# Attention and gated feed-forward in one kernel: the start of the first block in another order, with up weights loaded early

## The chip, the cores and the metric

The kernel runs on one core of a Trainium2 chip. The metric is device time in microseconds; the median of several executions counts. TensorE (PE) multiplies, VectorE (DVE) and ScalarE (ACT) do elementwise work and copy results out of PSUM, GpSimd (POOL) does masks and scaling, SyncE (SP) issues most of the DMAs.

## The reference, cut to what matters

One input x of 2048 tokens by 448 features is normalized, and the result feeds two branches: sliding-window attention with 16 heads of 28 features and a window of 256 tokens, and a gated feed-forward of width 1792. All tensors are bf16.

```python
xn = _layernorm(x)                       # x: (1, 2048, 448)
qkv = (xn @ wqkv)                        # wqkv: (448, 3 * 448), 16 heads of 28
scores = einsum("bhqd,bhkd->bhqk", q, k) * 28 ** -0.5
scores = where((i - j >= 0) & (i - j < 256), scores, -1e9)
attn = einsum("bhqk,bhkd->bhqd", softmax(scores), v) @ wo
ffn = (gelu(xn @ w_gate) * (xn @ w_up)) @ w_down      # w_gate, w_up: (448, 1792)
return x + attn + ffn
```

## The kernel before

The tokens are cut into 16 tiles of 128 and four blocks (`qb`) of 512. `stat(t)` takes mean and variance of a tile on DVE, `rstd(t, n)` the inverse deviation of n tiles on ACT (logarithm, then exponential), `norm(t)` writes the normalized tile `xn`. The transposed form `xnT` comes for tiles 0 to 3 from PE (`transp`: four transposes into PSUM and a copy), for later tiles from a DMA transpose issued by SP (`dma_transp`).

The 448 features are three chunks of 128 rows and a last one of 64. A product over them is therefore three dense matmuls (`mm3`) and one of half height (`mm_half`). `norm` writes the last 64 features twice, so that two half matmuls, of two different results, can run side by side in the upper and the lower half of the PE array. This text calls a stretch of half-height matmuls between dense ones an excursion.

Every block has an attention stage and a gated stage. In attention, each of four groups of heads has score steps (`sc`, four heads side by side, 32 rows each), an exponential of the scores on ACT into `p_sb`, masks on POOL (block 0) or DVE, and later the product with v (`ov`). Block 0 has twelve score steps, three in each group: 512, 384 and 256 columns of each head. The score pool has one buffer of four PSUM banks, so a score step waits until the exponential before it is done.

Between score steps PE is filled from `feeds`, lists of generators taken in order: `gen_qk` (q and k of a head group), `gen_v` (v of two tiles), `gen_proj` (all projections of the next block), `gen_up` (up products of two rows of 128 hidden features, `ue`, kept in hT until the gate is there). `bank()` gives these results PSUM banks in turn from a ring of tags: m (two banks) and d; tag o has one bank. A result's bank is free again when ACT or DVE has copied it out. `aux` holds one call after each score step, such as statistics of later tiles. The order of each engine's instructions is the order in which the program writes them; nothing is moved by a scheduler afterwards.

The first block starts with an order written out by hand: warm-up matmuls on zeros, the statistics, norms and transposes of tiles 0 to 3, v of tiles 0 and 1, q and k of group 0 in two halves of 256 tokens, v of tiles 2 and 3. Then the loop over blocks begins, and its first feed goes on with q and k of groups 1 to 3, the projections of block 1 and two up pairs (`early`).

The weights of q and k come by DMA as `wraw` and are copied by `pads` into `wqp` and `wkp`, where each head has 32 columns; the last 64 rows of q and k go to `w3p`. DMAs take one of eight completion semaphores in turn, so that a DMA issue waits until the one eight before it has landed. `loads()` issues the DMA transposes of tiles 4 to 7 and then the loads of up, gate, wo and down weights, after the second score step.

Of the kernel before, what the change touches and what calls it, by code (L numbers as in the profile page):

```python
# [12 lines left out]
f32 = mybir.dt.float32  # L13
# [3 lines left out]
P = 128  # L17
# [58 lines left out]
def kernel(  # L76
# [21 lines left out]
    def score_pool(n):  # L98

        if phase[0] is not None:  # L100
            phase[0].close()
        phase[0] = ExitStack()
        phase[0].pool = phase[0].enter_context(tc.tile_pool(name="sps", bufs=n, space=bass.MemoryType.PSUM))

    score_pool(1)
# [17 lines left out]

    nc.sync.dma_start(out=x_sb[:, 0, :], in_=xv[:, 0, :])
    nc.scalar.dma_start(out=x_sb[:, 1, :], in_=xv[:, 1, :])
    nc.sync.dma_start(out=x_sb[:, 2:4, :], in_=xv[:, 2:4, :])
    nc.sync.dma_start(out=wv[:, 0:3, :], in_=rows(A_wqkv, 0, 3)[:, :, 2 * D:3 * D])
    nc.scalar.dma_start(out=wraw[:, 0:3, :], in_=rows(A_wqkv, 0, 3)[:, :, 0:2 * D])
    for a in range(2):
        nc.sync.dma_start(out=wv[64 * a:64 * a + 64, 3, :], in_=A_wqkv[384:448, 2 * D:3 * D])  # L130
    for a in range(2):
        nc.sync.dma_start(out=wraw[64 * a:64 * a + 64, 3, 0:D], in_=A_wqkv[384:448, a * D:(a + 1) * D])
    nc.sync.dma_start(out=x_sb[:, 4:8, :], in_=xv[:, 4:8, :])

# [4 lines left out]
    nc.sync.dma_start(out=x_sb[:, 8:16, :], in_=xv[:, 8:16, :])  # L139
# [16 lines left out]
    make_masks()  # L156
# [20 lines left out]
    def warmup(n):  # L177
        wps = phase[0].pool.tile([P, 4, QB], f32, name="wps", tag="s")
        for i in range(n):
            nc.tensor.matmul(wps[:, i % 4, :], lhsT=warm[:, 0:P], rhs=warm[:, 0:QB], start=True, stop=True)  # L180
# [14 lines left out]
    def norm(t):  # L195
        xn = work.tile([P, 4, P], bf16, name="xn", bufs=4)
        xf = xn[:, :, :].rearrange("p a b -> p (a b)")
        for eng, lo, n, src in ((nc.vector, 0, D, 0), (nc.vector, D, 64, 384)):
            eng.tensor_scalar(out=xf[:, lo:lo + n], in0=x_sb[:, t, src:src + n], scalar1=mv_all[:, t, 0:1],
                              scalar2=rstd_all[:, t:t + 1], op0=ALU.subtract, op1=ALU.mult)  # L200
        xns[t] = xn
# [33 lines left out]

    def gen_v(qb, ts):

        for t in ts:
            pvs = []
            for i in range(2):  # L240
                pv = bank("pv")
                cs = slice((t + i) * P, (t + i + 1) * P)
                mm3(pv[:, 0:D], lambda c: xnT[:, c, cs], lambda c: wv[:, c, :], True, False)
                pvs.append(pv)
                yield (570, HOLD) if i else 570
            for i in range(2):
                mm_half(pvs[i][:, 0:D], xnT[:, 3, (t + i) * P:(t + i + 1) * P], wv[:, 3, :], i, False, True)
            for i in range(2):
                (nc.vector.tensor_copy if qb > 1 or i else nc.scalar.copy)(out=v_sb[:, t + i, :, 0:Dh], in_=pvs[i][:, 0:D].rearrange("p (h d) -> p h d", d=Dh))  # L249
            yield -360  # L250

    def gen_qk(qb, gs, lo=0, n=QB):

        ts = slice(qb * QB + lo, qb * QB + lo + n)
        for g in gs:
            hs = slice(4 * g, 4 * g + 4)
            pq = bank("pq")
            mm3(pq[:, 0:n], lambda c: wqp[:, c, hs, :].rearrange("p h d -> p (h d)"), lambda c: xnT[:, c, ts], True, False)
            yield 650
            pk = bank("pk")  # L260
            mm3(pk[:, 0:n], lambda c: wkp[:, c, hs, :].rearrange("p h d -> p (h d)"), lambda c: xnT[:, c, ts], True, False)
            yield 650, HOLD
            w3 = w3p[:, hs, :].rearrange("p h d -> p (h d)")
            mm_half(pq[:, 0:n], w3, xnT[:, 3, ts], 0, False, True)
            mm_half(pk[:, 0:n], w3, xnT[:, 3, ts], 1, False, True)
            nc.scalar.copy(out=qT[:, g, ts], in_=pq[:, 0:n])
            nc.vector.tensor_copy(out=kT[:, g, ts], in_=pk[:, 0:n])  # L267
            if lo + n == QB:
                done.add((qb, g))
            yield -360  # L270
# [67 lines left out]
    def gated(qb, early, last_v, hook):  # L338
# [5 lines left out]
        def begin(f):  # L344
            last_tag[0] = turn[0] if f not in early else last_tag[0]
            pr = dict(f=f, gt=phase[0].pool.tile([P, 2, QB], f32, name="gt", tag="s"), us=[])
            if f not in early:
                alone = (turn.pop(0), 1)
                tags = (("m", 2), alone)
                if qb == 0 and f == 0:  # L350
                    nxt = [ring[0][(ring[1] + i) % 3] for i in range(2)]
                    tags = [(x, 2 if x == "m" else 1) for x in nxt]
                for tag, n in tags:
                    pr["us"].append(psum.tile([P, QB], f32, name="u0", tag=tag, bufs=n))
            return pr
# [244 lines left out]
    warmup(10)  # L600
# [5 lines left out]
    transp(0, 1, nc.scalar.copy, "o")  # L606
    norm(1)
    warmup(1)
    transp(1, 1, nc.scalar.copy, "d")
    stat(2)  # L610
    stat(3)
    rstd(2, 2)
# [3 lines left out]
    norm(2)  # L616
    norm(3)
    run(gen_v(0, (0,)))
    qk = gen_qk(0, (0,), 0, 2 * P)
    next(qk)  # L620
    transp(2, 1, nc.scalar.copy, "o")
    transp(3, 1, nc.vector.tensor_copy, "m")
    stat(4)
    run(qk)
    stat(5)
    pads(nc.vector.tensor_copy, wqp, slice(1, 4))
    pads(nc.vector.tensor_copy, wkp, slice(1, 4))
    run(gen_qk(0, (0,), 2 * P, 2 * P))
    rstd(4, 2)
    stat(6)  # L630
    v23 = gen_v(0, (2,))
    next(v23)
    next(v23)
    norm(4)
    norm(5)
    stat(7)

    def loads():

        for t in range(4, 8):  # L640
            dma_transp(t)
        nc.sync.dma_start(out=wu[:, :, :], in_=rows(B_w_up, 0, 3))
        for t3, lo, hi in ((wgu3, B_w_gate, B_w_up), (wug3, B_w_up, B_w_gate)):
            nc.sync.dma_start(out=t3[0:64, :], in_=lo[384:448, :])
            nc.sync.dma_start(out=t3[64:128, :], in_=hi[384:448, :])
        for lo in (0, F // 2):
            nc.sync.dma_start(out=wg[:, :, lo:lo + F // 2], in_=rows(B_w_gate, 0, 3)[:, :, lo:lo + F // 2])
        wo_v = A_wo.rearrange("(g j d) n -> j d g n", g=4, j=4)
        for j in range(4):
            nc.sync.dma_start(out=wo[32 * j:32 * j + Dh, :, :], in_=wo_v[j])  # L650
        for k in range(0, NF, 3):
            n = min(3, NF - k)
            nc.sync.dma_start(out=wd[:, k:k + n, :], in_=rows(B_w_down, k, n))

    for qb in range(NB):
        early = ()
        aux, plan = [], {}
        if qb < 2:
            aux = [lambda: rstd(6, 2), lambda: (norm(6), norm(7), loads()), lambda: None] * (1 - qb) + [lambda t=t: stat(t) for t in range(8, 12)] * (1 - qb) + [lambda: rstd(4 * qb + 8, 4)]
        if qb == 0:  # L660
            new_hT(0)
            early = (2, 8)
            feeds = [Feed((v23, 360), (gen_qk(0, (1, 2, 3)), 3 * QK1), (gen_proj(1), PROJ), (gen_up(0, early), UP1 * len(early)))]
            feeds[0].held = True
# [12 lines left out]
        if qb:  # L677
            score_pool(1)
# [157 lines left out]
```

## Time and profile before

| | |
|---|---|
| median of 5 runs | 228.19 us (227.95 to 228.72) |
| profiled execution | 228.19 us |
| its span, first to last instruction | 226.2 us |
| PE, DVE, ACT, POOL busy | 217.1, 147.6, 133.4, 43.2 us |
| mean granted PE clock | 0.995 |
| DMA moved | 12.69 MB, 56 GB/s over the span |

The span leaves out some 2 us around the instructions. PE's busy time counts pipelined matmuls whose ends are modelled, so it can be 96% while PE still loses time between starts; the starts of its instructions tell more. A line number such as L218 is the line of the kernel, but helpers such as `mm3` record all their matmuls under one line, so the tile names (pv for v, pq and pk for q and k, sc for scores, ue and u for up, gt for gate, po for the output) tell which work it is.

### The profile page before, as it was taken

To read this page: it belongs to the slowest core of one execution; us is meant where nothing else is said; L and a number is where in the kernel's file an instruction comes from. 1 tells how busy PE (TensorE), PEld (TensorE's weight loads), DVE (VectorE), ACT (ScalarE), POOL (GpSimd) and SP (SyncE) were. 2 spreads that over 40 slices of the span, in tenths; PEclk is the share of its full clock that TensorE was granted. 3 is DMA by queue.
4 is the path that set the end of the run, shared out by engine and by line. 5 is a ranking of instruction groups with operands and counts; after the bars stand their busy time and mean duration, and the time that the engine had idled before them with its cause. 6 is when DMAs were issued, how large, how long until landed. Compare 5 with 4: busy or idle time off the path is not lost.

```text
span 226.2 us, 5435 instructions
## 1 busy us (share of the span) xinstructions
PE 217.1 (96%) x2262; PEld 97.0 (43%) x2262; DVE 147.6 (65%) x353; ACT 133.4 (59%) x129; POOL 43.2 (19%) x63
## 2 busy tenths in 40 slices
PE   6889999999999999999999999999999999999990
PEld 2433333344444444444444445444344435334470
DVE  5896887777675647588565656595444776679310
ACT  4578897524868876422868886333567775653000
POOL 8514777320000002222000002222000002222000
PEclk9999999999999999999999999999999999999997
DMA  6916999211200001001300100000000000100011
GB/s 215 328 28 74 313 311 308 74 23 31 44 0 24 25 5 41 6 0 38 59 0 23 24 4 25 23 0 0 0 4 23 22 5 5 42 3 0 22 45 26
DMA packets 18454, 12.69 MB, mean 56 GB/s; under 512 B 9784, under 2 KB 17784, under 8 KB 18424
## 3 DMA queue, kind: packets, MB, share of 16 engines
q1 hardware_dynamic: 17880, 11.48, 19.0%
q10 hardware_dynamic: 544, 0.80, 1.0%
q8 instruction: 19, 0.31, 0.6%
q14 instruction: 11, 0.09, 0.2%
HBM read 8.77 MB, written 1.84 MB: 47 GB/s over the span
## 4 chain that ended last, share of the span: by engine, by line
PE 86%; DVE 5%; ACT 2%; DMA 2%; SPq 1%; POOL 1%; issue 1%; DVEq 0%
PE po L301 19%; PE gt L218 16%; PE u L218 11%; PE po L296 6%; PE sc L539 6%; PE gt L223 5%; PE ov L501 4%; PE ue L218 4%; PE pq L218 4%; PE pk L218 4%; PE pv L218 3%; DMA wraw<-in_A_wqkv_dram 2%; PE pq L223 2%; POOL oN L451 1%; PE ue L223 1%; DVE st L185 1%
## 5 line engine op out<-in xcount | busy, mean ns | idle before, releaser
L543 ACT ACTIVATE p_sb<-sc 128x2048 bf16<-128x2048 f32 (+2 forms) x42 | 73.9, 1759 | 10.2 <-PE sc L539 8.5
L301 PE MATMUL po<-wd,hT 128*128 128x448 bf16 (+1 forms) x238 | 50.0, 342 | 0.0
L376 ACT ACTIVATE ge<-gt 128x1024 bf16<-128x1024 f32 x28 | 28.7, 1024 | 35.4 <-PE u L223 22.2
L218 PE MATMUL gt<-xnT,wg 128*128 128x512 bf16 x168 | 40.5, 380 | 0.0
L451 POOL TENSOR_TENSOR oN<-oc,rb 128x512 bf16<-128x512 f32 x10 | 12.7, 1269 | 118.0 <-DVE ri L480 62.1
L380 DVE TENSOR_TENSOR hT<-ge,u 128x512 bf16<-128x512 bf16 x42 | 26.9, 682 | 11.8 <-ACT ge L376 11.7
L218 PE MATMUL u<-xnT,wu 128*128 128x512 bf16 x126 | 30.6, 379 | 0.0
L301 PEld LDWEIGHTS <-hT 128*128 128x128 bf16 x238 | 21.6, 98 | 18.6 <-issue 2.2
L432 DVE TENSOR_TENSOR p_sb<-p_sb,masks 128x256 bf16<-128x256 bf16 (+1 forms) x90 | 24.6, 329 | 0.0
L218 PEld LDWEIGHTS <-wg 128*128 128x128 bf16 x168 | 15.1, 98 | 21.6 <-issue 5.4
L218 PEld LDWEIGHTS <-wu 128*128 128x128 bf16 x168 | 16.0, 98 | 19.2 <-issue 1.0
L507 DVE TENSOR_TENSOR oc<-oc,ov 128x512 f32<-128x512 f32 x12 | 8.3, 688 | 19.4 <-ACT oc L506 19.4
L539 PE MATMUL sc<-qT,kT 32*64 32x320 bf16 (+7 forms) x640 | 16.9, 263 | 0.4 <-ACT p_sb L543 0.3
L442 POOL TENSOR_SCALAR_AFFINE_SELECT p_sb<-p_sb 128x512 bf16<-128x512 bf16 (+1 forms) x20 | 14.2, 727 | 13.3 <-ACT p_sb L543 13.3
L306 DVE TENSOR_TENSOR res<-po,x_sb 128x448 bf16<-128x448 f32 (+1 forms) x17 | 9.9, 584 | 10.4 <-PE po L301 10.1
L296 PE MATMUL po<-wo,oN 128*128 128x448 bf16 (+1 forms) x68 | 16.3, 343 | 0.0
L267 DVE CAST kT<-pk 128x512 bf16<-128x512 f32 (+1 forms) x17 | 11.0, 648 | 7.8 <-PE pk L223 7.8
L506 ACT COPY oc<-ov 128x512 f32<-128x512 f32 x12 | 7.0, 585 | 15.2 <-POOL oN L451 12.8
L451 POOL TENSOR_TENSOR oN<-oc,l 128x512 bf16<-128x512 f32 x6 | 8.4, 1394 | 30.7 <-DVE l L468 30.7
L335 DVE CAST hT<-ue 128x512 bf16<-128x512 f32 x14 | 9.0, 686 | 7.1 <-PE ue L223 7.1
L223 PE MATMUL gt<-xnT,wgu 64*128 64x512 bf16 x49 | 13.6, 380 | 0.1
L218 PE MATMUL pq<-xnT,wqp 128*128 128x512 bf16 (+1 forms) x51 | 13.2, 368 | 0.2 <-DVE v_sb L249 0.2
(75 smaller groups left out, 236.4 us busy)
## 6 DMA issues: line engine op xcount, KB each, us to landing
out_dram<-res SPq DMA_DIRECT2D x15, 112.0 KB, 1.9
wu<-in_B_w_up_dram SPq DMA_DIRECT2D x1, 1344.0 KB
wg<-in_B_w_gate_dram SPq DMA_DIRECT2D x2, 672.0 KB, 9.6
wd<-in_B_w_down_dram SPq DMA_DIRECT2D x4, 336.0 KB, 7.3
x_sb<-in_A_x_dram SPq DMA_DIRECT2D x1, 896.0 KB, 5.8
wraw<-in_A_wqkv_dram ACTq DMA_DIRECT2D x1, 672.0 KB, 5.1
x_sb<-in_A_x_dram SPq DMA_DIRECT2D x1, 448.0 KB
wo<-in_A_wo_dram SPq DMA_DIRECT2D x4, 98.0 KB
```

The lines of the kernel that those rows point to most:

```text
L218: nc.tensor.matmul(ps, lhsT=lhs(c), rhs=rhs(c), start=start and c == 0, stop=stop and c == 2, skip_group_check=True)
L223: nc.tensor.matmul(ps, lhsT=lhs[p0:p0 + 64], rhs=rhs[p0:p0 + 64], start=start, stop=stop, tile_position=(p0, 0), skip_group_check=True)
L267: nc.vector.tensor_copy(out=kT[:, g, ts], in_=pk[:, 0:n])
L296: nc.tensor.matmul(po[:, 0:w], lhsT=oN[:, g, cs], rhs=wo[:, g, lo:up], start=(g == 0), stop=False, skip_group_check=True)
L301: nc.tensor.matmul(po[:, 0:w], lhsT=hT[:, f, cs], rhs=wd[:, f, lo:up], start=False, stop=(f == NF - 1), skip_group_check=True)
L376: nc.scalar.activation(out=ge[:, :, :], in_=pr["gt"][:, :, :], func=ACT.Gelu_apprx_tanh)
L380: nc.vector.tensor_tensor(out=hT[:, f + i, :], in0=ge[:, i, :], in1=u[:, :], op=ALU.mult)
L432: nc.vector.tensor_tensor(out=reg, in0=reg, in1=m, op=ALU.mult)
L442: nc.gpsimd.affine_select(out=reg, in_=reg, pattern=mid + [[1 if diag else -1, min(w, P)]], compare_op=ALU.is_ge, fill=0.0, base=0 if diag ...
L451: nc.gpsimd.tensor_tensor(out=oN[:, g, :], in0=oc[:, :], in1=inv, op=ALU.mult)
L539: nc.tensor.matmul(ss[k0:k0 + nk, j, col:col + nq], lhsT=kT[r, g, kt * P + k0:kt * P + k0 + nk], rhs=qT[r, g, qb * QB + q0:qb * QB + q0 + ...
L543: nc.scalar.activation(out=p_sb[:, :, 0:ncol], in_=ss[:, :, 0:ncol], func=ACT.Exp, scale=SCALE)
```

## The change

The start of block 0 is written in another order, and with it some loads and the score pool.

- v of a tile is put behind the transposes of the next one, with its dense part alone (`v_dense`). The half-height parts of q and k of group 0 and of v of tiles 0 and 1 stand together in one excursion; those of v of tiles 2 and 3 are added to the excursion of group 1's q and k.
- q and k of group 0 are computed for all 512 tokens at once, in the score pool, which begins as two buffers of two banks and becomes one of four when the scores begin.
- `rstd` runs for tiles 2 and 3 one by one; the second 64 features' copy of tiles 1 and 2 is written by POOL; `make_masks` comes later on POOL; eight warm-up matmuls open the kernel instead of ten.
- ACT's queue loads only group 0's columns of q and k; the others come on SP's queue, and the last rows of wraw go ahead of those of wv. Up weights are loaded ahead of x of tiles 8 to 11; x of tiles 12 to 15 and the gate, wo and down weights follow in `loads()`, some in fewer DMAs.
- Norms and transposes of tiles 4 to 7, and v's copies of tiles 2 and 3, are spread over the first score steps (`ahead`, `ahead2`, `ahead3`).
- One up pair stands ahead of block 1's projections in the feed, the other behind them.

```diff
-    score_pool(1)
+    score_pool(2)
...
+    wqk = rows(A_wqkv, 0, 3)[:, :, 0:2 * D]
     nc.sync.dma_start(out=x_sb[:, 0, :], in_=xv[:, 0, :])
     nc.scalar.dma_start(out=x_sb[:, 1, :], in_=xv[:, 1, :])
     nc.sync.dma_start(out=x_sb[:, 2:4, :], in_=xv[:, 2:4, :])
+    for c in (0, D):
+        nc.scalar.dma_start(out=wraw[:, 0:3, c:c + 4 * Dh], in_=wqk[:, :, c:c + 4 * Dh])
     nc.sync.dma_start(out=wv[:, 0:3, :], in_=rows(A_wqkv, 0, 3)[:, :, 2 * D:3 * D])
-    nc.scalar.dma_start(out=wraw[:, 0:3, :], in_=rows(A_wqkv, 0, 3)[:, :, 0:2 * D])
+    for a in range(2):
+        nc.sync.dma_start(out=wraw[64 * a:64 * a + 64, 3, 0:D], in_=A_wqkv[384:448, a * D:(a + 1) * D])
     for a in range(2):
         nc.sync.dma_start(out=wv[64 * a:64 * a + 64, 3, :], in_=A_wqkv[384:448, 2 * D:3 * D])
-    for a in range(2):
-        nc.sync.dma_start(out=wraw[64 * a:64 * a + 64, 3, 0:D], in_=A_wqkv[384:448, a * D:(a + 1) * D])
     nc.sync.dma_start(out=x_sb[:, 4:8, :], in_=xv[:, 4:8, :])
+    for c in (0, D):
+        nc.sync.dma_start(out=wraw[:, 0:3, c + 4 * Dh:c + D], in_=wqk[:, :, c + 4 * Dh:c + D])
...
-    nc.sync.dma_start(out=x_sb[:, 8:16, :], in_=xv[:, 8:16, :])
+    nc.sync.dma_start(out=wu[:, :, :], in_=rows(B_w_up, 0, 3))
+    nc.sync.dma_start(out=wug3[0:64, :], in_=B_w_up[384:448, :])
+    nc.sync.dma_start(out=wgu3[64:128, :], in_=B_w_up[384:448, :])
+    nc.sync.dma_start(out=x_sb[:, 8:12, :], in_=xv[:, 8:12, :])
...
-        for eng, lo, n, src in ((nc.vector, 0, D, 0), (nc.vector, D, 64, 384)):
+        for eng, lo, n, src in ((nc.vector, 0, D, 0), (nc.gpsimd if t in (1, 2) else nc.vector, D, 64, 384)):
...
+    def v_dense(t, pv):
+        mm3(pv, lambda c: xnT[:, c, t * P:(t + 1) * P], lambda c: wv[:, c, :], True, False)
+
+    def v_half(t, pv):
+        mm_half(pv, xnT[:, 3, t * P:(t + 1) * P], wv[:, 3, :], t % 2, False, True)
+
+    def v_copy(t, pv, copy):
+        copy(out=v_sb[:, t, :, 0:Dh], in_=pv.rearrange("p (h d) -> p h d", d=Dh))
...
+    def qk_halves(qb, g, pq, pk):
+        w3 = w3p[:, 4 * g:4 * g + 4, :].rearrange("p h d -> p (h d)")
+        for hi, ps in enumerate((pq, pk)):
+            mm_half(ps, w3, xnT[:, 3, qb * QB:(qb + 1) * QB], hi, False, True)
...
                     nxt = [ring[0][(ring[1] + i) % 3] for i in range(2)]
                     tags = [(x, 2 if x == "m" else 1) for x in nxt]
+                    if "d" in nxt:
+                        turn.insert(0, "o")
...
-    warmup(10)
+    warmup(8)
     stat(0)
     rstd(0, 1)
     stat(1)
     rstd(1, 1)
     norm(0)
     transp(0, 1, nc.scalar.copy, "o")
+    stat(2)
     norm(1)
+    rstd(2, 1)
     warmup(1)
     transp(1, 1, nc.scalar.copy, "d")
-    stat(2)
     stat(3)
-    rstd(2, 2)
+    rstd(3, 1)
+    pvs = [bank("pv")[:, 0:D]]
+    v_dense(0, pvs[0])
+    norm(2)
     pads(nc.vector.tensor_copy, wqp, slice(0, 1))
     nc.vector.tensor_copy(out=w3p[:, :, 0:Dh], in_=wraw[:, 3, 0:D].rearrange("p (h d) -> p h d", d=Dh))
     pads(nc.scalar.copy, wkp, slice(0, 1))
-    norm(2)
+    transp(2, 1, nc.scalar.copy, "o")
+    pvs.append(bank("pv")[:, 0:D])
+    v_dense(1, pvs[1])
     norm(3)
-    run(gen_v(0, (0,)))
-    qk = gen_qk(0, (0,), 0, 2 * P)
-    next(qk)
-    transp(2, 1, nc.scalar.copy, "o")
-    transp(3, 1, nc.vector.tensor_copy, "m")
+    make_masks()
+    transp(3, 1, nc.vector.tensor_copy, "d")
+    pvs.append(alone("pv", "o"))
+    v_dense(2, pvs[2])
+    pq, pk = (phase[0].pool.tile([P, 2, QB], f32, name="s0", tag="s")[:, 0, :] for _ in range(2))
+    proj(pq, wqp, 0, 0)
+    proj(pk, wkp, 0, 0)
     stat(4)
-    run(qk)
     stat(5)
-    pads(nc.vector.tensor_copy, wqp, slice(1, 4))
-    pads(nc.vector.tensor_copy, wkp, slice(1, 4))
-    run(gen_qk(0, (0,), 2 * P, 2 * P))
     rstd(4, 2)
-    stat(6)
-    v23 = gen_v(0, (2,))
...
+    qk_halves(0, 0, pq, pk)
+    for t in range(2):
+        v_half(t, pvs[t])
+    qk_copies(0, 0, pq, pk)
+    for dst in (wqp, wkp):
+        pads(nc.vector.tensor_copy, dst, slice(1, 2))
+    v_copy(0, pvs[0], nc.scalar.copy)
+    v_copy(1, pvs[1], nc.vector.tensor_copy)
+    pvs.append(alone("pv", "d"))
+    v_dense(3, pvs[3])
+    ring[1] = 0
+    for dst in (wqp, wkp):
+        pads(nc.vector.tensor_copy, dst, slice(2, 4))
+
+    def ahead():
+        norm(4)
+        dma_transp(4)
+
+    def ahead2():
+        stat(6)
+        stat(7)
+        rstd(6, 2)
+        norm(5)
+        dma_transp(5)
+
+    def ahead3():
+        for t in (6, 7):
+            norm(t)
+            dma_transp(t)
+        v_copy(2, pvs[2], nc.vector.tensor_copy)
+        loads()
...
-            feeds = [Feed((v23, 360), (gen_qk(0, (1, 2, 3)), 3 * QK1), (gen_proj(1), PROJ), (gen_up(0, early), UP1 * len(early)))]
-            feeds[0].held = True
+            feeds = [Feed((gen_qk(0, (1, 2, 3), [(t, pvs[t]) for t in (2, 3)]), 3 * QK1 + 360), (gen_up(0, early[0:1]), UP1), (gen_proj(1), PROJ), (gen_up(0, early[1:]), UP1))]
```

## The prediction

> **What bounds the kernel now.** I read the page first, then what TensorE (PE) waited for, then PE's timeline over the first 27 us.
>
> ```profile
> span 226.2 us, 5435 instructions
> ...
> PE 217.1 (96%) x2262; PEld 97.0 (43%) x2262; DVE 147.6 (65%) x353; ACT 133.4 (59%) x129; POOL 43.2 (19%) x63
> ...
> PE   6889999999999999999999999999999999999990
> ...
> PE 86%; DVE 5%; ACT 2%; DMA 2%; SPq 1%; POOL 1%; issue 1%; DVEq 0%
> ```
>
> PE is the bound: 86% of the chain that ended last, and its row of tenths is below 9 only in the first three slices (17 us) and the last. The change moves work in the first block only, so what it can bring is in these three slices. What PE waited for, longest first:
>
> ```profile
> PE wps L180 <- DVE wo L160: 2.0, 1, 2.0
> PE pv L218 <- DMA wv<-in_A_wqkv_dram: 1.0, 1, 1.0
> PE sc L539 <- ACT p_sb L543: 0.3, 1, 0.3
> PE pq L218 <- DVE v_sb L249: 0.2, 1, 0.2
> ```
>
> Little is recorded as a wait. More is seen from start to start. PE's timeline (start, length, operation, in brackets the idle time before it):
>
> ```profile
> 1.96 4.04 PE L180 MATMUL wps<-wo 128*128 128x512 bf16 x10 [1.96 <-DVE wo L160]
> ...
> 7.63 1.29 PE L218 MATMUL pv<-wv,xnT 128*128 128x448 bf16 x6 [0.96 <-DMA wv<-in_A_wqkv_dram]
> 8.86 0.36 PE L223 MATMUL pv<-wv,xnT 64*128 64x448 bf16 x2
> ...
> 10.30 0.49 PE L218 MATMUL pk<-xnT,wkp 128*128 128x256 bf16 x3
> ...
> 11.46 0.49 PE L218 MATMUL pk<-xnT,wkp 128*128 128x256 bf16 x3
> ...
> 13.67 0.40 PE L539 MATMUL sc<-qT,kT 32*128 32x128 bf16 x8
> ...
> 16.10 0.34 PE L539 MATMUL sc<-qT,kT 32*128 32x384 bf16 x4 [0.31 <-ACT p_sb L543]
> 16.68 0.81 PE L218 MATMUL pq<-xnT,wqp 128*128 128x512 bf16 x3 [0.24 <-DVE v_sb L249]
> ...
> 18.56 0.29 PE L539 MATMUL sc<-qT,kT 32*128 32x256 bf16 x4
> ...
> 26.87 0.40 PE L539 MATMUL sc<-qT,kT 32*128 32x128 bf16 x8
> ```
>
> Prices from it. Six dense ue matmuls start at 33.79 and their half-height pair at 35.19: 0.216 us for a 512-column matmul plus about 0.105 for the change of shape; likewise 0.19 for 448 columns. A pair of halves runs together, and the next operation starts 0.32 later (0.215 + 0.105). So an excursion to half height costs two changes, 0.21 us. From 7.63 to 26.87 the matmuls at these prices are 14.76 us, 27 changes of shape 2.82, and what is left of the 19.24, 1.66 us, is waiting: about 0.3 before each of the two pk, 0.38 before the scores at 16.10 and 0.31 after them, 0.17 before those at 18.56. After 20.5 PE runs through, so a lead won before is kept to the end, unless something later is late.
>
> **The change part by part.** I compare where PE stands at the seventh score step (sc at 26.87). Up to there the new order has one up pair (ue) in place of one q/k group of block 1; both cost 6 dense and 2 half matmuls (1.72), and the rest behind is the same work.
>
> 1. Excursions. Before: v of tiles 0,1; q/k twice in 256-column halves; v of 2,3: four, of which one turns straight into the scores: nine changes of shape up to q/k of group 1. After: one for q, k, v0, v1, then v3 dense, scores: four. The last rows of v2, v3 go into group 1's excursion. Five changes at 0.105 are **-0.52 us**. The columns are equal: six 256-column matmuls twice are six of 512.
>
> 2. An earlier start. v dense began at 7.63, when wv landed; its xnT was ready at 6.90 (its weight load). wv shared the DMA engines with 672 KB of wraw; now only 168 KB go ahead on that queue, in pieces of 224 bytes. Between 8 and 10 us the loads ran at 802 packets, most of 896 bytes, in 2 us:
>
> ```profile
> DMA packets 802, 0.70 MB, mean 352 GB/s; under 512 B 16, under 2 KB 802, under 8 KB 802
> ```
>
> That is 40 ns a packet on each of 16 engines. 768 small pieces cost between a quarter of that (by bytes, 0.5 us over 16 engines) and all of it (1.9 us, which is what the 672 KB took at 352 GB/s). By the trace I take some 25 ns, 1.2 us: wv lands at 6.2 to 6.8, and v starts at 6.88, set by the transposes: **-0.75 us**. The Trainium skill speaks against this ("DMA: Bandwidth & Descriptors", Specifications): below 512 B a transfer is a read-modify-write and not at line rate. By that rule I let a small piece cost as much as a whole packet: wv stays at 7.63, but the waits behind it shrink (tile 1 is ready by then), and the sum is 0.8 us instead of 1.1. A gain either way; at 100 ns a piece wv would be at 8.6 and nothing gained. I take the trace's nearest row and keep the rule for the range.
>
> 3. The chain behind it, walked with DVE's and ACT's start-to-start times: statistics of a tile 0.755, norm 0.51, 448-wide alone 0.34, q or k copy 0.48 on ACT and 0.60 on DVE, v copy 0.43 and 0.52, exp 1.80, 1.37, 0.95, transposed copy 0.49 and 0.34, padding 0.2 to 0.3, and 0.05 from an end to a waiting start. The same walk over the kernel before meets its scores within 0.1 us from 13.67 to 24.92. After: xn of tile 1 waits behind statistics of tile 2 (6.25, transposed 6.66); tile 2's transposes 7.75, tile 3's 8.70, v2 8.97; q/k of all 512 tokens at 9.56, once xnT of tile 3 is copied; halves 10.96; q copied by 12.15, scores 12.15 (before 13.67). Then ACT has 7.1 us of exp and copies against PE's 6.0 for three q/k groups and their scores, and DVE is full: group 2's q waits 0.49 for the d bank, which v3's copy on DVE frees at 15.2 (queued behind paddings and norm 4); group 3's k waits 0.58 for group 2's q copy, queued on ACT behind the rstd of tiles 6,7, which waits for DVE's statistics (17.4). The scores stand at 14.51, 16.98, 19.50 (before 16.10, 18.56, 20.51), 22.15, 24.02 and 25.77. New waits sum to 1.83 against 1.66: **+0.17 us**. So half of the lead of 1.5 us at 12.15 is given back.
>
> Sum: -0.52 - 0.75 + 0.17 = **-1.1 us** at the seventh score step.
>
> 4. POOL takes two 64-wide norms. No row shows that operation; the nearest, affine_select on 64x64, is 0.24 us, the dearest POOL row near it, tensor_tensor 128x512, 1.27. I take 0.45, hidden: tile 1's runs at 5.55 while DVE is in statistics until 6.25. At 1.3 it would cost 0.35. DVE saves two of 0.2, counted above. make_masks (memset 0.76, 18 selects in 5.04) now ends near 13.2; the first score mask is wanted at 14.5, the masks in block 1. Without that cover POOL would pay the difference, and PE only at the ov products.
>
> 5. Queues. SP issues twelve loads ahead of the transposes instead of eight, at 0.6 us each: 2.4 more, over by 11 or so, and the first transpose is wanted at 14.1. ACT issues one more (0.46), its table load ends at 3.5 rather than 3.0; its first logarithm is at 4.28. Up weights and the rest land by 16 at 350 GB/s (4.3 MB from 2.0 on with the small pieces); up is used at 19.8, and wraw's rest, landing near 10.5, at 12.0. Transposes of tiles 4 to 7 stand behind these loads on SP's queue: asked for at 14.1, 17.9, 19.1, 20.3, with 2.6 to 4.1 us to land as before, so the last at 24.4 at worst, used at 24.8. Each of these covers is nil above its margin: 4, 1.5 and 0.4 us, then microsecond for microsecond.
> Gate and down weights (one and two issues instead of two and five) are asked for no later than before and used at 39.6 and 60.0: nothing. Swapped banks o and d in the up stage: the copy of the last ov product frees o at 43.5, wanted at 44.1: nothing, up to 0.3 if late.
>
> 6. Eight warm-up matmuls instead of ten. The first ones cost 0.43 us, then 0.22:
>
> ```profile
> 4.92 0.15 PEld L180 LDWEIGHTS <-wo 128*128 128x128 bf16 x1 [0.28 <-issue]
> 5.35 0.15 PEld L180 LDWEIGHTS <-wo 128*128 128x128 bf16 x1 [0.28 <-issue]
> 5.62 0.43 PEld L213 LDWEIGHTS <-xn 128*128 128x128 bf16 x4
> ```
>
> Weight loads are 0.43 apart up to 5.35; the transposes start at 5.84, so the last two warm-ups together took 0.46. PE speeds up at 5.38, 3.42 us after its start, though the granted clock is given as 1.00 throughout. Eight matmuls end at just 5.38. By the row PE is fast from there: nothing lost. "TensorE: Matmul & The Clock Gate" (Trainium skill, Part 1) says that the gate opens after a busy window of about 3.4 us which runs freely, and Part 4 that transposes do not count as busy; by this rule the gate may open one window later, at 8.8, since PE then is idle more than half the time. Walked at half speed until 8.8, the seventh score step is at 26.88: the whole 1.1 us gone. I follow the row.
>
> **The rivals.**
> - Forecast, 0.52: about -1.1 us; with the small unknowns 226.5 to 227.7.
> - Small pieces dear and wv no earlier, 0.16: 227.4 at the rule's price, up to 228.2. For: 224 bytes, four DMAs now ahead of or beside wv. Against: a fifth of the bytes.
> - Clock gate, 0.12, the one that ends slower. One window late gives 228.2; two (12.2 us) put the seventh step at 28.1, +1.2: 229.4. It is slower as soon as the gate stays shut past 8.8. For: two warm-ups gone, gaps of 0.7 and 0.3 us between the first products. Against: the speed-up at 5.38 comes before the two last warm-ups were done.
> - A late arrival, 0.12: wraw's rest after 12.0 or transposes past 24.4: each further microsecond is one; 228.0 to 229.
> - The change not doing what it says, 0.08: DVE's and ACT's queues return the lead entirely by the third score step (7.1 us of ACT work is the limit there): 227.7 to 228.2.
>
> **How the numbers follow.** The profiled execution took 228.19 for a span of 226.2, and 228.19 is also the median, so 228.19 - 1.1 = 227.1. About 0.2% (0.46 us) is what a measurement of this kernel can tell from no change: faster is below 227.7, slower above 228.7. Faster: 0.52 of the forecast, 0.08 of the dear pieces, 0.05 of the rest: 0.65. Same: 0.06, 0.06, 0.05 and 0.01 of the rivals: 0.18. Slower: 0.02, 0.06, 0.06 and 0.03: 0.17. The range 226.4 to 228.6 leaves out what gate and late arrivals put above, and a little below.
>
> **What would show it.** First v product near 6.9, scores at 12.2, 14.5, 17.0, 19.5, seventh step near 25.8. Wrong if v starts at 7.6 or later (pieces), if matmuls before 9 us start 0.4 apart (gate), if group 1's q or v of tiles 6,7 waits for a DMA (late arrival), or if the fourth score step is no earlier than 20.5 (queues). If the seventh step is a microsecond ahead and the end isn't, a later stage took it.

## The result, and the profile after

The changed kernel takes 227.2 us in the median of 31 runs (226.38 to 227.91); the kernel before took 228.02 in 52 runs beside it (227.3 to 228.93). The ratio is 0.9961, with an interval of 0.9952 to 0.9969: 0.9 us less, where 1.1 had been forecast. The profiled execution of after took 226.45 us for a span of 224.7. It is the second fastest of the 31, and that of before (228.19) lies a little above its median, so the two profiles differ by 1.74 us, more than the medians do.

The page of after, in the rows that were shown of before:

```profile
span 224.7 us, 5422 instructions
...
PE 216.1 (96%) x2252; PEld 95.5 (42%) x2252; DVE 148.6 (66%) x353; ACT 132.9 (59%) x129; POOL 44.4 (20%) x65
...
PE   6899999999999999999999999999999999999991
...
PE 88%; DVE 5%; ACT 1%; POOL 1%; DMA 1%; issue 1%; DVEq 0%
```

PE still bounds it, now with 88% of the chain. The third slice of its row went from 8 to 9 tenths; nothing else in the row moved but the last digit. That agrees with a gain before 17 us, where it was looked for; the starts below show it. What PE waited for in after, without the 2.0 at its very start (total, times, longest, in us):

```profile
PE tp L219 <- DVE xn L205: 0.8, 2, 0.6
PE pk L224 <- ACT qT L276: 0.4, 1, 0.4
PE pq L224 <- DVE v_sb L249: 0.3, 1, 0.3
```

The wait for wv (1.0 before) is gone. In its place the transposes wait for DVE (0.8), and two waits of the third step of the prediction are there by name: group 3's k for the copy of group 2's q, and group 2's q for v's copy. PE's timeline of after (start, length, operation, in brackets the idle time before it):

```profile
6.85 0.73 PE L224 MATMUL pv<-wv,xnT 128*128 128x448 bf16 x3
...
11.09 0.39 PE L229 MATMUL s<-xnT,w3p 64*128 64x512 bf16 x2
...
11.60 0.74 PE L224 MATMUL pv<-wv,xnT 128*128 128x448 bf16 x3
12.30 0.40 PE L567 MATMUL sc<-qT,kT 32*128 32x128 bf16 x8
...
14.73 0.34 PE L567 MATMUL sc<-qT,kT 32*128 32x384 bf16 x4
15.34 0.81 PE L224 MATMUL pq<-xnT,wqp 128*128 128x512 bf16 x3 [0.27 <-DVE v_sb L249]
...
17.05 0.29 PE L567 MATMUL sc<-qT,kT 32*128 32x256 bf16 x4
...
18.45 0.81 PE L224 MATMUL pk<-xnT,wkp 128*128 128x512 bf16 x3 [0.36 <-ACT qT L276]
...
25.82 0.40 PE L567 MATMUL sc<-qT,kT 32*128 32x128 bf16 x8
```

v starts at 6.85 instead of 7.63, the first scores at 12.30 instead of 13.67, the seventh score step at 25.82 instead of 26.87. The lead is 1.37 us at the first scores and 1.05 at the seventh step. It is 1.14 at the last matmul group (218.29 against 219.43); the other 0.6 by which the two profiles differ lies behind that group.

### The profile page after: what moved, and what is told of

It reads as the page before. It is cut to its first block, busy times and chain, and to the rows that moved or that the text cites. A ratio compares the mean times of both kernels' runs of the same rounds, so it can differ in the third digit from the quotient of the medians.

```text
span 224.7 us, 5422 instructions
## 1 busy us (share of the span) xinstructions
PE 216.1 (96%) x2252; PEld 95.5 (42%) x2252; DVE 148.6 (66%) x353; ACT 132.9 (59%) x129; POOL 44.4 (20%) x65
## 4 chain that ended last, share of the span: by engine, by line
PE 88%; DVE 5%; ACT 1%; POOL 1%; DMA 1%; issue 1%; DVEq 0%
PE po L327 19%; PE gt L224 16%; PE u L224 12%; PE po L322 6%; PE sc L567 6%; PE gt L229 5%; PE ov L529 4%; PE ue L224 4%; PE pk L224 4%; PE pq L224 4%; PE pv L224 4%; PE pq L229 2%; DVE st L191 1%; POOL oN L479 1%; DMA x_sb<-in_A_x_dram 1%; PE ue L229 1%
## 5 line engine op out<-in xcount | busy, mean ns | idle before, releaser
L277 DVE CAST kT<-pk 128x512 bf16<-128x512 f32 x15 | 10.2, 683 | 6.5 <-PE pk L229 6.5
L224 PE MATMUL pk<-xnT,wkp 128*128 128x512 bf16 x45 | 12.2, 379 | 0.4 <-ACT qT L276 0.4
```

What stands on the lines that cost most here:

```text
L224: nc.tensor.matmul(ps, lhsT=lhs(c), rhs=rhs(c), start=start and c == 0, stop=stop and c == 2, skip_group_check=True)
L277: nc.vector.tensor_copy(out=kT[:, g, ts], in_=pk)
```

## The experiments

All were timed beside the kernel before: the first four on one chip, the next four on a second, the last four on a third, so that across these groups only the ratios can be compared. For each profile I give two marks, the start of the first scores (sc1) and of the seventh score step (sc7); before has 13.67 and 26.87, after 12.30 and 25.82. A ratio is to the kernel before.

| kernel | sc1 | sc7 | last matmul group | median | ratio and interval |
|---|---|---|---|---|---|
| new order, old loads | 12.61 | 26.13 | 218.72 | 227.69 | 1.0004 [0.9980, 1.0028] |
| old order, new loads | 13.38 | 26.51 | 219.54 | 228.10 | 1.0007 [0.9995, 1.0019] |
| one more excursion | 12.57 | 26.52 | 219.22 | 227.33 | 0.9974 [0.9964, 0.9985] |
| no early up pair | 12.28 | 31.43 | 224.27 | 230.78 | 1.0114 [1.0082, 1.0145] |
| four warm-ups | 13.14 | 26.67 | 218.94 | 227.50 | 0.9968 [0.9952, 0.9984] |
| ten warm-ups | 12.88 | 26.40 | 218.93 | 227.00 | 0.9956 [0.9941, 0.9971] |
| early memset | 11.82 | 25.57 | 218.49 | 227.00 | 0.9952 [0.9933, 0.9971] |
| late rstd | 12.31 | 25.77 | 218.45 | 226.82 | 0.9940 [0.9919, 0.9961] |
| the changed kernel again | 12.31 | 25.90 | 218.44 | 226.81 | 0.9958 [0.9940, 0.9975] |
| both mends | 11.98 | 25.21 | 217.85 | 226.53 | 0.9940 [0.9926, 0.9954] |
| both, and statistics later | 12.10 | 25.10 | 217.87 | 225.80 | 0.9910 [0.9895, 0.9925] |
| norms off POOL | 12.29 | 25.81 | 218.38 | 226.57 | 0.9940 [0.9925, 0.9954] |

**1. New order with the old loads.** The first loads of before, in before's order, under the new order of the block:

```diff
-    for c in (0, D):
-        nc.scalar.dma_start(out=wraw[:, 0:3, c:c + 4 * Dh], in_=wqk[:, :, c:c + 4 * Dh])
+    nc.scalar.dma_start(out=wraw[:, 0:3, :], in_=rows(A_wqkv, 0, 3)[:, :, 0:2 * D])
...
     # the last rows of wv ahead of those of wraw, and no later load of the other columns
```

> The changed kernel with the loads of v, q and k weights as before: one DMA of all 672 KB of wraw on ACT's queue beside wv, the last rows of wv ahead of those of wraw. Theory (the start of v moved earlier because wv no longer shares the DMA engines with 672 KB): wv lands at about 7.6 instead of 6.8, v starts 0.75 us later, but the waits behind it shrink, so the seventh score step is 0.3 us later (26.1) and the time about 0.3 us over the changed kernel, 227.5. Rival (the reordering alone carries the gain, the load is hidden): v starts at 7.6, and the scores at 12.3 do not move. Rival (small pieces are dear, the old load is as good or better): v starts no later than 6.9.

sc7 is 0.31 later than in after, as expected, and so is sc1. But the reason was not the one expected: v starts at 7.11, 0.26 later than in after and not 0.75. DVE's timeline names what else is late:

```profile
7.39 0.27 DVE L619 COPY wqp<-wraw 128x336 bf16<-128x336 bf16 x1
7.87 0.83 DVE L646 COPY w3p<-wraw 128x448 bf16<-128x448 bf16 x1 [0.21 <-DMA wraw<-in_A_wqkv_dram]
8.62 0.60 DVE L202 TENSOR_SCALAR xn<-x_sb,mv_all,rstd_all 128x448 bf16<-128x448 bf16 x2
```

The copy of the last rows (w3p) waits for its load, and norm 3 stands behind it: 8.62, where after has 8.31, the same 0.31 that the scores lose. So the order of the loads is worth 0.3 us in the profile, by way of w3p on DVE.

The time says more than the profile. The ratio, 1.0004, lies with its whole interval above that of after (0.9952 to 0.9969): without the new loads the new order can't be told from the kernel before. Two of the twelve executions took 229.54 and 229.71 us, at a mean granted clock of 0.991 and 0.990 where the others have 0.994 to 0.999. That is what a stretch at half clock would give, such as experiment 4 shows, but there is no profile of these two. The other ten alone are at 0.9987, still 0.6 us above after. What costs these tenths is open.

**2. Old order with the new loads**, the reverse edit on the kernel before.

> The kernel before with only the new loads of v, q and k weights (group 0's columns in 224-byte pieces on ACT's queue, the rest on SP's, last rows of wraw ahead of those of wv). Theory: v starts at 6.8 instead of 7.6; the chain of norms, transposes and statistics on DVE then holds PE, and the sixth score step comes 0.3 us earlier (24.6): 0.3 us faster than before, 227.7. Rival (the early start is worth its whole 0.75 us by itself): 24.2 and 227.3. Rival (loads are hidden): no change.

v starts at 6.88 instead of 7.63 and still the scores start only 0.29 earlier, the seventh step 0.36 earlier; the sixth step, 24.56, is where the theory put it. An early v is worth little by itself: the rest of the 0.75 is lost again on the way to the first scores. In the time nothing shows (1.0007). Its last matmul group even starts 0.11 later than in before; "What was not expected" tells where such tenths go. In the profiles the two experiments add up: loads 0.31 to 0.36, order 0.69 to 0.74 at sc7, together 1.05. In the times they do not: either half alone is at the time of before, and only both together are 0.9 us faster.

**3. One more excursion.** One of v3's dense matmuls is put between the half-height parts of q/k and those of v, which costs two more changes of shape and no other work:

```diff
     qk_halves(0, 0, pq, pk)
+    pvs.append(alone("pv", "d"))
+    v3((0,))
     for t in range(2):
         v_half(t, pvs[t])
...
-    v_dense(3, pvs[3])
+    v3((1, 2))
```

> The changed kernel with its one excursion split: one dense matmul of v of tile 3 stands between the half matmuls of q, k and those of v of tiles 0 and 1, so two more changes of shape, the same matmuls. Theory (each change costs 0.105 us and PE sets the pace there): the first score step 0.21 us later (12.51), and the time 0.2 us over the changed kernel, 227.4. Rival (DVE's chain of copies and statistics, then ACT, sets the pace until the fourth score step): the first score step 0.2 later, but group 3's k and the fourth score step (19.51) within 0.1 us of the changed kernel, and no change of time.

```profile
11.17 0.39 PE L229 MATMUL s<-xnT,w3p 64*128 64x512 bf16 x2
11.49 0.36 PE L667 MATMUL pv<-wv,xnT 128*128 128x448 bf16 x1
11.79 0.36 PE L229 MATMUL pv<-wv,xnT 64*128 64x448 bf16 x2
12.08 0.55 PE L667 MATMUL pv<-wv,xnT 128*128 128x448 bf16 x2
12.57 0.40 PE L567 MATMUL sc<-qT,kT 32*128 32x128 bf16 x8
...
23.80 0.74 PE L224 MATMUL pv<-wv,xnT 128*128 128x448 bf16 x3 [0.35 <-DMA xnT<-xn]
```

From the q/k halves to the scores it takes 1.40 us, against 1.21 in after (11.09 to 12.30): 0.19 for two changes, 0.095 each, where the prediction had 0.105. The fourth score step is 0.26 later too (19.77), which rules out the rival, that VectorE and ScalarE set the pace until there. The whole loss at sc7 is larger, 0.70, and the last line shows most of the rest: in this execution v of tile 5 waited 0.35 us for its DMA transpose. That transpose was asked for at 18.50 and used at 23.80, over 5 us later. This is a first sight of how thin the cover of the transposes is.

**4. No early up pair.** Both up pairs stand behind block 1's projections, as in before:

```diff
-feeds = [Feed((gen_qk(...), ...), (gen_up(0, early[0:1]), UP1), (gen_proj(1), PROJ), (gen_up(0, early[1:]), UP1))]
+feeds = [Feed((gen_qk(...), ...), (gen_proj(1), PROJ), (gen_up(0, early), 2 * UP1))]
```

> The changed kernel with both early up pairs behind block 1's projections, as in the kernel before; the up weights are still loaded early. Theory (the up pair covers the DMA transposes of tiles 4 to 7, which come later than before): v of tile 5 waits for its transpose (asked for at 18.2, landing 20.6) and v of tile 7 for its own (asked for at 22.0, landing 24.4) against uses at 20.4 and 22.9: 1.5 us slower than the changed kernel, 228.7. Rival (the transposes land in time, the place of the up pair is of no account): no wait on a DMA, no change.

```profile
19.83 0.74 PE L224 MATMUL pv<-wv,xnT 128*128 128x448 bf16 x3
23.49 1.30 PE L224 MATMUL pv<-wv,xnT 128*128 128x448 bf16 x3 [2.92 <-DMA xnT<-xn]
24.72 0.56 PE L229 MATMUL pv<-wv,xnT 64*128 64x448 bf16 x2
25.21 1.15 PE L529 MATMUL ov<-p_sb,v_sb 128*32 128x128 bf16 x16
```

Without the pair PE comes to tile 5 three microseconds too early and stands idle for 2.92 us, until the transpose asked for at 18.21 has landed. Then it pays again: three v matmuls take 1.30 instead of 0.74, the ov products 1.15 instead of 0.67, until about 29 us. Over the same stretch, from 22.6 to 29.3, the granted clock is 0.50. The seventh step comes 5.6 us late, where the theory had 1.5. This profile is of the longest of six executions (232.48), which the ratio leaves out; the shortest took 228.89, so not every one lost so much. By the other five the kernel is still 1.1% slower than before: without the early up pair the change loses.

**5. Four warm-ups, and ten**, instead of eight (`warmup(4)`, `warmup(10)`).

> The changed kernel with four warm-up matmuls instead of eight. Clock-gate theory (a busy stretch of about 3.4 us opens the gate): PE is busy from 1.96 to 3.7 only, matmuls still start 0.4 us apart in the first products of v, and the gate opens after 8.8: the first score step at 13.3 or later, the time 1 us or more over the changed kernel, 228.3. Rival (warm-ups are of no account, the chain of DVE and ACT hides a slow PE): the first score step within 0.3 us of 12.3, no change of time.

> The changed kernel with ten warm-up matmuls as before. Theory (eight are enough, the gate opens near 5): the two more delay tile 0's transposes from 5.25 by 0.2 to 0.5 us, v still waits for tile 1's transposes and wv (6.8): no change of time beyond 0.1 us. Clock-gate theory (with eight, some executions open the gate late): ten are faster by 0.2 us or more in the median, and the slowest executions are fewer.

With four, PE's matmuls stay at half pace until 9.5:

```profile
6.93 1.33 PE L224 MATMUL pv<-wv,xnT 128*128 128x448 bf16 x3
...
8.47 1.33 PE L224 MATMUL pv<-wv,xnT 128*128 128x448 bf16 x3
...
9.87 0.73 PE L224 MATMUL pv<-wv,xnT 128*128 128x448 bf16 x3
```

That profile loses 0.84 at sc1 and 0.85 at sc7, and its execution (227.29) took 0.84 us more than the profiled one of after (226.45). But that one is among after's fastest, and 227.29 is below the median with four: the ratios, 0.9968 with four and 0.9961 with eight, can't be told apart. So the theory had the late scores nearly right and the rival the time. With ten the time is that of eight too (0.9956); in the profiled execution (227.61, above its median) the extra two ran at half pace and delayed the first transposes to 6.17. No difference between the counts shows in the medians; when the other executions came to full pace is not known.

**6. Early memset.** In after, two of DVE's copies are three times as long as in before (0.89 and 0.82 against 0.24 and 0.28). They ran while POOL filled the masks with ones. The memset is moved out of `make_masks`, back to where POOL does it before the first block:

```diff
     masks = const.tile([P, 3, 4, 64], bf16, name="masks")
+    nc.gpsimd.memset(masks[:, :, :, :], 1.0)
     def make_masks():
-        nc.gpsimd.memset(masks[:, :, :, :], 1.0)
```

> The changed kernel with the memset of masks on POOL ahead of the two 64-wide norms instead of behind them. In the changed kernel two DVE copies (wqp and w3p) took 0.89 and 0.82 us while that memset ran, against 0.24 and 0.28 before. Theory (POOL's memset holds DVE's copies up): the copies take 0.25 again, tile 3's norm starts 0.3 us earlier (8.0), q of group 0 at 9.45 instead of 9.70, all scores 0.25 us earlier and the time 0.25 us less, 226.95. Rival (the copies waited for the weights' DMA): they end at 8.3 as before, no change.

DVE and POOL in after, then in this kernel:

```profile
3.34 0.63 DVE L191 BATCH_NORM_STATS2 st<-x_sb 128x6 f32<-128x448 bf16 x1 [1.18 <-DMA x_sb<-in_A_x_dram]
...
7.38 0.89 DVE L622 COPY wqp<-wraw 128x336 bf16<-128x336 bf16 x1
7.57 0.82 DVE L649 COPY w3p<-wraw 128x448 bf16<-128x448 bf16 x1
8.31 0.59 DVE L205 TENSOR_SCALAR xn<-x_sb,mv_all,rstd_all 128x448 bf16<-128x448 bf16 x2
...
7.35 0.85 POOL L154 MEMSET masks<- 128x768 bf16 x1
```

```profile
3.14 0.63 DVE L192 BATCH_NORM_STATS2 st<-x_sb 128x6 f32<-128x448 bf16 x1 [0.99 <-DMA x_sb<-in_A_x_dram]
...
7.19 0.27 DVE L623 COPY wqp<-wraw 128x336 bf16<-128x336 bf16 x1
7.37 0.28 DVE L650 COPY w3p<-wraw 128x448 bf16<-128x448 bf16 x1
7.78 0.65 DVE L206 TENSOR_SCALAR xn<-x_sb,mv_all,rstd_all 128x448 bf16<-128x448 bf16 x2
...
3.52 0.76 POOL L153 MEMSET masks<- 128x768 bf16 x1
```

The copies are back at 0.27 and 0.28, and q/k (9.22 instead of 9.70) and the first scores start 0.48 earlier. But 0.20 of this was there before the copies: in this execution x landed earlier, so that DVE's first statistics start at 3.14 instead of 3.34. From these statistics to q/k it takes 6.08 us here and 6.36 in after. The memset is worth the difference, 0.28, near the 0.25 expected; the kernel "both" of experiment 8 takes 6.08 too. About half of the 0.48 is lost again before sc7 (-0.25): v of tile 5 waits for its bank, which the first copy of the up pair frees on DVE, behind the statistics of tile 8.

**7. Late rstd.** The logarithm of tiles 6 and 7 waits for their statistics and holds group 2's q copy behind it on ACT. It is issued one score step later, after norm 5 and its transpose:

```diff
     def ahead2():
-        stat(6)
-        stat(7)
-        rstd(6, 2)
         norm(5)
         dma_transp(5)
+        stat(6)
+        stat(7)
     def ahead3():
+        rstd(6, 2)
```

> The changed kernel with the rstd of tiles 6 and 7 one score step later on ACT (behind group 2's q copy and exp), and norm and transpose of tile 5 ahead of the statistics of tiles 6 and 7 on DVE. Theory (group 3's k waits because group 2's q copy is queued on ACT behind that rstd, which waits for DVE): the q copy starts at 17.2 instead of 17.8, group 3's k at 17.9 instead of 18.45, the fourth score step at 19.0, and the time 0.5 us less, 226.7. Rival (another wait takes its place: v of tiles 6 and 7 for transposes that are now later, or the ov product for v's copy on DVE): the fourth score step is earlier but the seventh is not.

ACT in after, then in this kernel:

```profile
17.40 0.29 ACT L196 ACTIVATE lnv<-mv_all,eps_t 128x2 f32<-128x2 f32 x1 [0.82 <-DVE mv_all L192]
...
17.83 0.57 ACT L276 CAST qT<-pq 128x512 bf16<-128x512 f32 x1
```

```profile
17.40 0.59 ACT L276 CAST qT<-pq 128x512 bf16<-128x512 f32 x1 [0.75 <-PE pk L229]
```

The q copy no longer stands behind the logarithm, group 3's k runs without its wait, and the fourth score step is 0.27 earlier (19.24), although the third is 0.25 later in this execution. For that DVE's timeline has a reason:

```profile
12.70 0.28 DVE L622 COPY wkp<-wraw 128x336 bf16<-128x336 bf16 x1 [0.27 <-DMA wraw<-in_A_wqkv_dram]
```

The rest of wraw came 0.27 us late for group 1's k. At sc7 0.05 is left: the rival was right that another wait takes the place of this one, but it is neither of the two that it named. It is v's wait for its bank, as in experiment 6 (six v matmuls take 1.61).

**8. Both mends, and then the wait that both ran into.** "Both" is 6 and 7 together. The last kernel has one empty place more in `aux`, so that the statistics of tiles 8 to 11 come one score step later and the up pair's copies stand ahead of tile 8's:

```diff
-            aux = [ahead, ahead2, ahead3] * (1 - qb) + ...
+            aux = [ahead, ahead2, ahead3, lambda: None] * (1 - qb) + ...
```

> Both mends that were tried singly: the masks' memset before the first block, and the logarithm and exponential of tiles 6 and 7 issued one score step later. Theory (the two waits are independent: the slow copies of VectorE delay q and k by 0.48, the early logarithm delays group 3's k by 0.4): q/k 9.2, scores 11.8, the fourth step at 18.7, seventh 25.4 to 25.6 because the early up pair's v copy then waits for the statistics of tile 8 on VectorE; time 226.6 to 226.8. Rival (both stand on the same next wait, VectorE's queue ahead of the up pair's copies): seventh step 25.6 or later, time no less than either alone, 226.9.

> Both mends, and the statistics of tiles 8 to 11 one score step later, so that the two copies of the early up pair stand ahead of tile 8's statistics in VectorE's queue. Theory (that queue is what both single mends ran into): fourth step at 18.5 to 18.7, v of tiles 4 and 5 without a wait for its bank, seventh step 25.0 to 25.2, 0.7 ahead of the changed kernel, time 226.4. Rival (the transpose of tile 5, which lands by DMA near 22.8, becomes the wait): v of tiles 4 and 5 waits for a DMA, seventh step 25.5, time 226.8.

PE in "both", then in the last kernel:

```profile
21.60 1.62 PE L225 MATMUL pv<-wv,xnT 128*128 128x448 bf16 x6
23.15 0.36 PE L230 MATMUL pv<-wv,xnT 64*128 64x448 bf16 x2
```

```profile
21.72 1.31 PE L225 MATMUL pv<-wv,xnT 128*128 128x448 bf16 x6
22.96 0.36 PE L230 MATMUL pv<-wv,xnT 64*128 64x448 bf16 x2
```

Six v matmuls take 1.62 with the wait inside them and 1.31 without. Together the two mends bring 0.61 at sc7 (25.21), more than the 0.25 and 0.05 that they brought singly, though in the time "both" (0.9940) can't be told from one mend. The third takes the last wait: sc7 at 25.10, from a first scores step that happened to be 0.12 later. The transpose of tile 5 did not become the wait, since mend 7 asks for it at 16.66 instead of 18.23. Time 225.8 us, 1.0 below the changed kernel on the same chip (226.81); the two intervals, 0.9895 to 0.9925 and 0.9940 to 0.9975, don't meet. This version beats both kernels. The time is 0.6 lower than expected, and the last matmul group is only 0.57 ahead of the changed kernel's on that chip: the profiles show a part of the 1.0, not all of it.

**9. Norms off POOL.** The 64-wide parts of tiles 1 and 2 are on DVE again (`nc.gpsimd if t in (1, 2) else nc.vector` becomes `nc.vector`).

> The changed kernel with the 64-wide parts of the norms of tiles 1 and 2 back on VectorE. Theory (the prediction's: they are 0.2 each on VectorE, on the path to xn of tile 1): transposes of tile 1 at 6.6 to 6.7 in place of 6.5, scores 12.4 to 12.6, seventh step 25.9 to 26.1, time +0.1 to +0.3, 227.4. Rival (TensorE starts the v product of tile 0 when wv lands, at 6.85, whatever tile 1 does, and POOL's part of tile 2 ends later than VectorE's would): scores at 12.1 to 12.3, time 227.1 to 227.2.

> The changed kernel unaltered, to stand beside the three others on one chip. Both theories: 227.2 us, 0.8 below the kernel before; in its profile the first v product near 6.9, scores at 12.3, 14.7, 17.05, 19.5, the seventh step at 25.8. If the start of the faster TensorE moves with the execution, as the last runs suggest, the first products may stand up to 0.5 later and the scores still at 12.3.

sc1 and sc7 are those of after (12.29 and 25.81), and the time is not above it. The number is the rival's, the reason is not. In this kernel POOL has nothing queued ahead of the masks, so the memset is back at 3.52 and DVE's copies take 0.27 and 0.26. x landed later in this execution (DVE's first statistics start at 3.47), so the stretches from there to q/k have to be compared: 6.22 us here, 6.36 in after, and 6.08 in experiment 6, where the norms are on POOL and the memset is early too. So the POOL norms are worth 0.14 us, but in the changed kernel they push the memset into DVE's copies, which costs 0.28: there, moving them lost more than it brought.

## Why the prediction was right, and where its steps were not

1. **Excursions.** The price was right: 0.095 a change of shape measured in one profile (experiment 3), 0.105 used. That five of them bring their whole 0.52 was not measured by itself.

2. **The earlier start of v.** The start itself was right (6.88 forecast, 6.85). The small pieces were cheaper than taken. Between 4 and 6 us, where 512 of the packets are small, after moved (all packets, then SP's queue q1 and ACT's queue q10: packets, MB, share of the 16 engines' time):

```profile
DMA packets 1094, 0.62 MB, mean 308 GB/s; under 512 B 512, under 2 KB 1094, under 8 KB 1094
q1 hardware_dynamic: 654, 0.52, 81.7%
q10 hardware_dynamic: 440, 0.09, 21.6%
```

ACT's queue carries the small pieces. Its share of 2 us on 16 engines is 6.9 us over 440 packets, 16 ns a packet where 25 were taken; on SP's queue it is 40. wv landed at 6.83. A price as the prediction drew it from the skill's rule, wv no earlier than 7.63, did not come. (Its 8.6 for 100 ns a piece does not follow from its own price: 768 pieces at 60 ns more are 2.9 us over 16 engines, not 1.0. Nothing rests on it.) But the term of -0.75 is wrongly placed. Experiment 2 gives v the early start alone and gets 0.29 at sc1. (The old loads don't fix v's start either: it was 7.63 in before and 7.11 in experiment 1.) What sets q/k in the new order is not v but DVE, whose copy of tile 3's xnT ends at 9.65. Three profiles of the new order with eight warm-ups show it: v of tile 1 starts at 7.76, 8.04 and 8.04, q/k at 9.70, 9.72 and 9.71. So the sum was near and its parts were not: at sc1 1.52 was forecast and 1.37 measured, and of that the loads bring 0.3 in the profiles and the order the rest. That the parts made up for each other is in part luck, and the times of experiments 1 and 2 say that neither part works without the other.

3. **The chain behind it.** The score steps were forecast at 12.15, 14.51, 16.98, 19.50, 22.15, 24.02 and 25.77; they came at 12.30, 14.73, 17.05, 19.51, 22.17, 24.07 and 25.82. Both new waits were there at the place named, and experiments 7 and 8 show that DVE's and ACT's queues, not PE, decide them. So the lead given back between 12 and 19.5 us was real: 1.37 at sc1, 1.00 at the fourth step. It is a third, not half: by the prediction's own times too the lead goes from 1.52 to 1.01.

4. **POOL.** Mis-sized: the norms took 0.58 and 0.72, within the bounds but above the 0.45, and they were hidden. What the step lacked is a neighbour. It asked what covers POOL, not what POOL does to DVE: the masks' memset, pushed behind the norms to 7.35, slowed DVE's copies, 0.28 us at q/k (experiment 6), and the norms bring only 0.14 (experiment 9). The walk took these paddings at 0.2 to 0.3 and came out only 0.14 early at q/k (9.56 against 9.70), so some other term of it must have been too long; which one stays open.

5. **Queues.** SP issues fourteen loads ahead of the transposes, not twelve (nine before, not eight), and was through with them at 9.7. In both profiles of after all loads landed in time; in experiment 7, with the same loads, wraw's rest came 0.27 late. The first transpose was asked for at 14.29 (14.1 forecast), but the last at 21.99 instead of 20.3, since SP was held 2.38 us at tile 6's. No transpose came late in the two profiles of the changed kernel, yet experiments 3 and 4 show how near that is: tile 5's transpose took 5.3 us there, not 2.6 to 4.1, and in after v of tile 5 starts 4.8 us after the asking. "Swapped banks: nothing, up to 0.3 if late" had the wrong sign. In before, u's first half-height matmul of the gated stage came apart from its gate partner (43.80 and 44.10); in after they run together at 42.76, and the halves take 0.76 us instead of 1.04. This is read from the traces alone.

6. **Warm-ups.** The row was the better guide, with eight as with ten. The opening does move: matmuls are fast from about 5 in after, from 6.4 in its second profile, from 7.5 in experiment 7, with eight warm-ups each. "TensorE: Matmul & The Clock Gate" (Trainium skill, Part 1) says that the window runs freely and that the moment varies for that reason, by half a microsecond either way in one place, between 6 and 14 slow matmuls of one kernel in another; here it moves by 2.5 us. That costs nothing while DVE sets q/k: sc1 stands at 12.30 or 12.31 in all three. A later opening costs: 0.85 at sc7 with an opening at 9.5 (experiment 5). The rival's mechanism is real, then, but was priced too dear: it had the whole 1.1 gone at 8.8, while at 9.5 the seventh step (26.67) is still ahead of before's.

## What to carry to other kernels

When a start is written out by hand, walk the queue of the engine that feeds TensorE, not TensorE's own: here a product could start 0.75 us earlier and bring 0.3, because VectorE's last copy set the next one. A wait that is taken away shows its worth only together with the next in line; each of two mends alone left little at the seventh step, and with a third they brought 0.7 there and 1.0 in the time. Before two profiles are compared, line them up at the last event that the edit can't have touched: here x landed up to 0.33 us earlier or later, more than some mends are worth. Filling that stands ahead of DMA-fed work is part of its timing: ask what arrives late if the filler goes or the engine gets there sooner.

## What was not expected of the hardware

- A memset on POOL slows copies on DVE: 0.24 and 0.28 us become 0.89 and 0.82 beside a memset of 128x768 bf16. "GPSIMD Engine Reference" (Trainium skill, Specifications) says that the two share their interfaces to SBUF and contend in DVE's two-port modes; no run here shows whether these copies ran in such a mode. The copies look as if they waited for the memset to end rather than ran slower: it ends at 8.20, they at 8.27 and 8.39. In the second profile of after the memset came at 7.83 and hit norm 3 instead (0.94 for two instructions that take 0.60); q/k was at the same place.
- Matmuls run at half pace again after a gap of 2.9 us (experiment 4). The granted clock shows it: it falls to 0.50 at 22.5, 2 us after PE's last matmul, sooner than after the idle window of about 3.4 us that "TensorE: Matmul & The Clock Gate" (Trainium skill, Part 1) names, and is back at 29.3. Of the half pace at the start it shows nothing: it is 1.00 there while matmuls start 0.43 us apart.
- A DMA transpose of one tile took 5.3 us to be of use (18.21 to 23.49 in experiment 4), with the next asked for 1.3 us behind it. In before they are as close together (18.23 and 19.52), and the slowest landed within 4.1. Why it took longer is open.
- Executions of one kernel differ by some tenths at two places that have nothing to do with the change. At the end of block 1's attention eight small DMAs, which spread the inverse sums, land between 25.8 and 26.6 us after that block's first scores. DVE waits for them, POOL's scaling for DVE, ACT's copy and last exponential for POOL, and PE's gate products for that. Before, and experiment 6:

```profile
84.52 0.01 DVE L489 LOAD_MASK_SELECT rb<-oc  x1 [1.50 <-DMA oc<-ri]
```

```profile
83.70 0.01 DVE L518 LOAD_MASK_SELECT rb<-oc  x1 [2.27 <-DMA oc<-ri]
...
88.24 1.45 PE L225 MATMUL gt<-xnT,wg 128*128 128x512 bf16 x6 [0.33 <-ACT p_sb L572]
```

With first scores at 58.69 and 57.10 these are 25.83 and 26.60 us after them, and block 1 takes 52.34 and 52.99 us up to block 2's first scores. The other place is behind the last matmul group, where 8.1 to 9.3 us remain to the reported time. Together they hide what a single profile gains: experiment 2 leads before by 0.36 at sc7 and ends 0.6 behind it. Why these DMAs land earlier or later is open.
